# Pooled attention with a gated expert layer on one core: query rows summed by an accumulating DMA, exponentials issued head by head, a new order table

## Chip, cores and metric

One core of a Trainium2 chip. The metric is device microseconds of one execution of the whole program; the median of three timed runs of the kernel before is 1115.62 us (1115.05 to 1115.63).

## What is computed

The first half is attention with pooled queries, for 8 batches and 8 heads, 1152 positions, head size 64. The second half is a layer of 4 causal attention experts on the 576 pooled positions, of which every position takes the best 2.

```
q_pool = q.reshape(B, H, S // 2, 2, D).mean(axis=3)
scores = (q_pool @ k.T) / sqrt(D);  scores -= max;  a = exp(scores)
x      = (a / (sum(a) + 1e-9)) @ v                      # 8 x 576 x 512
logits = x @ w_gate                                     # best 2 of 4, softmax over them
for e in range(4):                                      # causal attention of expert e
    ye   = softmax(causal((x @ wq[e]) @ (x @ wk[e]).T / 8)) @ (x @ wv[e]) @ wo[e]
    out += gate[e] * ye
```

The mean over two query rows is computed as a sum; the factor of one half goes into the scale of the exponential (0.0625 where the reference has 0.125).

## The kernel before

Two heads make a pair, and 32 pairs (p) are worked off one after the other. A pair's two heads lie in the two halves of the 128 partitions. Precision is kept by splitting each fp32 operand into a high part in fp32r (`qh`, `kh`) and the rest (`ql`, `kl`); three products and one row that subtracts the maximum make a score.

For every pair:

- SyncE loads the raw queries `qraw` (both rows of each pooled pair: 128 partitions x 2 x 576, one buffer), the raw keys `kraw` in three pieces (512, 512, 128; the first pair in 3 x 384) and the values `v` in three (`f_loadq`, `f_loadk`, `f_loadv`).
- `f_prepq` makes `qh` and `ql` in two pieces of 256 and 320 columns: VectorE sums the two query rows into a PSUM bank (L559), ScalarE casts that to `qh` (L388) and copies a 64x64 corner into `QD`, VectorE subtracts `qh` from the bank and writes `ql` (L392). Only then is the bank free.
- `f_prepk` makes `kh` on ScalarE (L388) and `kl` on GpSimd (L396).
- `f_max` and `f_mxs` compute the scores of high parts alone on TensorE (L377, L368) and VectorE takes their row maxima (L633). `f_rows` turns these into the row `RM`.
- `f_st` computes the transposed scores (L377, four terms for each of 9 key chunks and 2 halves of the queries, `QB` = 256 and 320 columns); ScalarE writes the exponentials into SBUF tiles `pt` (L723). In the half of 256 columns two chunks share a PSUM bank per head, so a group is two chunks and two heads, four exponentials; in the other half it is one chunk and two heads.
- `f_av` multiplies them with `v` (L384); GpSimd adds the `pt` tiles of a half up (`pool_tt`, L396), or VectorE folds some of them into `part` instead (`fold_in`, L774). `f_xfin` and `g_norm` divide by the sum and write `x` as high and low part.

After every fourth pair one batch of the expert layer starts, and is worked off between the pairs that follow (`start_moe`; its exponentials are at L1104 and its causal mask is on GpSimd at L1124). The last batch has only the tail of the program beside it.

TensorE works in three arrangements, and the letters are those of the code: A, two row halves (L377); B, two column halves (L384, L821); C, the full array (L368).

The order of all instructions is set while the program is written. Each piece of work is a generator (`Flow`), and a planner in the main loop keeps a modelled clock for each engine (`emit`), with costs and semaphore delays as constants. It takes the next piece by readiness, arrangement and priority; the priorities come from a table of tuples, `PLAN`, of which a row applies to half a pair of progress (`row`). A booked DMA lands, in the planner, 0.65 us + bytes / 250 GB/s + 1.0 us after its issue. Each engine then runs its own list in that order, and waits where it must.

Of the kernel before, what the change touches and what calls it, by code (L numbers as in the profile page):

```python
# [1316 lines left out]
```

## Time and profile before

| what | value |
|---|---|
| median of three runs | 1115.62 us |
| the profiled execution, its own time | 1115.2 us |
| its span, first to last instruction | 1113.5 us |
| TensorE busy | 1090.7 us, 98% |
| VectorE busy | 925.1 us, 83% |
| GpSimd busy | 821.6 us, 74% |
| ScalarE busy | 655.4 us, 59% |
| DMA queue of SyncE | 68.29 MB, 19.1% of 16 engines' span |

The time is 1.7 us longer than the span. A matmul on two halves is two instructions that run side by side, so its rate is read from the start of one pair to the start of the next, and the busy times of neighbours overlap. A wait that TensorE sees at the weights of the next matmul (PEld) is in part hidden behind the matmul that still runs.

### The profile page before, as it was taken

Reading aid. Unit: us, or ns where it says so; the run is one execution under the profiler, and the core shown is the slowest. Engines: PE = TensorE matmul, PEld = TensorE weight load, DVE = VectorE, ACT = ScalarE, POOL = GpSimd, SP = SyncE. Lnnn points to the kernel's source line nnn. Section 1 sums busy time; section 2 is a strip of 40 time slices with the busy share of each in tenths; the row PEclk is TensorE's granted clock in tenths of the full one; section 3 lists DMA queues with packets and bytes.
Section 4 is the critical chain, followed back from the end, with each engine's and each line's share of the span. In section 5 each row is a group of like instructions: output and inputs, shape, how many; then the busy total and the mean of one; then the engine's idle time right before and its main releaser. Section 6 shows DMA issues by size and latency. Waiting matters only on the chain.

```text
span 1113.5 us, 29538 instructions
## 1 busy us (share of the span) xinstructions
PE 1090.7 (98%) x11184; PEld 877.2 (79%) x11184; DVE 925.1 (83%) x2159; ACT 655.4 (59%) x2067; POOL 821.6 (74%) x759
## 2 busy tenths in 40 slices
PE   6999999999999999999999999999999999999997
PEld 5777798778987888777887878778888867987785
DVE  8999969888798877988879787887888888685876
ACT  4776637575375744667446674567636766366534
POOL 4699948999189981999739996489865999278812
PEclk9999999999999999999999999999999999999999
DMA  5232202222021221212212031130221213010011
GB/s 168 83 117 84 89 32 66 66 66 85 20 81 51 63 84 41 78 44 66 84 40 89 24 101 47 51 108 2 94 74 66 66 26 123 22 31 2 1 39 48
DMA packets 41903, 70.32 MB, mean 63 GB/s; under 512 B 6688, under 2 KB 25120, under 8 KB 41760
## 3 DMA queue, kind: packets, MB, share of 16 engines
q1 hardware_dynamic: 41616, 68.29, 19.1%
q8 instruction: 88, 1.44, 0.5%
q14 instruction: 55, 0.45, 0.1%
q10 hardware_dynamic: 144, 0.13, 0.0%
HBM read 58.73 MB, written 9.44 MB: 61 GB/s over the span
## 4 chain that ended last, share of the span: by engine, by line
PE 84%; DVE 9%; POOL 3%; ACT 2%; issue 1%; DMA 0%; SPq 0%; DVEq 0%; POOLq 0%; ACTq 0%
PE gen L377 39%; PE gen L384 26%; PE gen L368 18%; DVE PM L633 3%; POOL pt L396 2%; ACT pt L723 2%; DVE gen L1060 1%; PE gen L821 1%; DVE part L774 1%; DVE pt L392 1%; POOL pt L1124 1%; DVE gen L836 1%; DMA qraw<-in_qT 0%; DVE gen L392 0%; DVE OL L392 0%
## 5 line engine op out<-in xcount | busy, mean ns | idle before, releaser
L396 POOL TENSOR_TENSOR pt<-pt,pt 128x512 f32<-128x512 f32 (+3 forms) x501 | 678.3, 1360 | 63.1 <-PE gen L384 17.1
L633 DVE TENSOR_REDUCE PM<-gen 128x1 f32<-128x512 f32 (+3 forms) x678 | 409.6, 658 | 84.9 <-PE gen L377 67.1
L723 ACT ACTIVATE pt<-gen 128x320 f32<-128x320 f32 (+1 forms) x1152 | 373.9, 435 | 57.7 <-PE gen L377 52.4
L384 PE MATMUL gen<-pt,v 128*64 128x320 f32 (+4 forms) x2752 | 343.9, 401 | 0.9 <-POOL pt L1124 0.7
L384 PEld LDWEIGHTS gen<-pt,v 128*64 128x64 f32 (+1 forms) x2752 | 187.9, 137 | 124.1 <-issue 4.3
L377 PE MATMUL gen<-qh,kh 64*128 64x320 f32 (+1 forms) x1152 | 238.2, 310 | 3.6 <-ACT pt L723 2.5
L377 PE MATMUL gen<-qh,kl 64*128 64x320 f32 (+1 forms) x1152 | 226.2, 299 | 0.0
L377 PE MATMUL gen<-RM,ON 64*128 64x320 f32 (+1 forms) x1152 | 217.5, 292 | 0.0
L377 PE MATMUL gen<-ql,kh 64*128 64x320 f32 (+1 forms) x1152 | 217.4, 292 | 0.0
L377 PEld LDWEIGHTS gen<-qh,kh 64*128 64x128 f32 x1152 | 162.8, 185 | 25.9 <-ACT pt L723 6.5
L377 PE MATMUL gen<-kh,qh 64*128 64x512 f32 (+2 forms) x768 | 151.9, 373 | 7.4 <-ACT qh L388 7.0
L377 PEld LDWEIGHTS gen<-ql,kh 64*128 64x128 f32 x1152 | 156.4, 186 | 0.0
L377 PEld LDWEIGHTS gen<-RM,ON 64*128 64x128 f32 x1152 | 156.3, 186 | 0.0
L377 PEld LDWEIGHTS gen<-qh,kl 64*128 64x128 f32 x1152 | 153.6, 186 | 2.6
L774 DVE TRANSPOSE_TENSOR_REDUCE part<-pt 128x20 f32<-128x640 f32 (+1 forms) x174 | 135.5, 789 | 17.9 <-POOL pt L396 17.7
L396 POOL TENSOR_TENSOR kl<-kraw,kh 128x512 fp32r<-128x512 f32 (+2 forms) x96 | 95.9, 1019 | 26.8 <-PE gen L377 23.1
L377 PEld LDWEIGHTS gen<-kh,qh 64*128 64x128 f32 x768 | 89.2, 188 | 25.5 <-issue 9.5
L975 POOL TENSOR_TENSOR gate<-v,gate 128x20 f32<-128x20 f32 x7 | 1.6, 231 | 144.9 <-DVE gate L975 144.9
L368 PE MATMUL gen<-x,WH 128*128 128x320 f32 (+1 forms) x512 | 105.0, 299 | 0.8 <-DVE x L392 0.8
L368 PEld LDWEIGHTS gen<-x,WH 128*128 128x128 f32 x512 | 82.1, 188 | 5.6 <-issue 3.0
L1060 DVE CUSTOM_DVE_ANT_0 gen<-gen,mqk 64x288 f32<-64x288 f32 (+4 forms) x160 | 74.1, 504 | 7.8 <-PE gen L377 6.7
L368 PE MATMUL gen<-x,WL 128*128 128x320 f32 (+1 forms) x256 | 75.6, 295 | 0.0
(120 smaller groups left out, 1472.7 us busy)
## 6 DMA issues: line engine op xcount, KB each, us to landing
v<-in_vP SPq DMA_DIRECT2D x96, 192.0 KB
qraw<-in_qT SPq DMA_DIRECT2D x31, 576.0 KB
kraw<-in_kT SPq DMA_DIRECT2D x62, 256.0 KB
out<-ob SPq DMA_DIRECT2D x28, 256.0 KB
kraw<-in_kT SPq DMA_DIRECT2D x31, 64.0 KB
RM<-nt SPq DMA_DIRECT2D x124, 1.2 KB
wst<-in_wall SPq DMA_DIRECT2D x8, 193.0 KB
MRM<-nt SPq DMA_DIRECT2D x56, 1.2 KB
```

The costliest lines, as they stand in the source:

```text
L368: nc.tensor.matmul(o, lhsT, rhs, start=start, stop=stop)
L377: nc.tensor.matmul(o(j), l(HEAD[j]), r(HEAD[j]), start=i == 0, stop=i == len(terms) - 1)
L384: nc.tensor.matmul(o(HEAD[j]), l(j), r(j), start=start, stop=stop)
L392: nc.vector.tensor_tensor(o, a, b, op=op)
L396: nc.gpsimd.tensor_tensor(o, a, b, op=op)
L633: nc.vector.tensor_reduce(pm[:, i:i + k, t], ps[:, :n * k].rearrange("p (c n) -> p c n", c=k), axis=AX.X, op=ALU.max)
L723: nc.scalar.activation(pts[i][:, j, :qn], st[j][:, qn * i:qn * i + qn], AF.Exp, scale=0.0625)
L774: nc.vector.tensor_reduce(out, src.rearrange("p a (b r) -> p a b r", r=32), axis=AX.X, op=ALU.add, apply_transpose=True)
L821: nc.tensor.matmul(den[HEAD[j], 400:400 + k], fold, part[:, m, j * k:j * k + k], start=True, stop=True)
L836: nc.vector.transpose(den[:, :n].rearrange("p (a b) -> p a b", b=32), r9[:, :k].unsqueeze(2).to_broadcast([128, k, 32]))
L1060: nc.vector.tensor_tensor_reduce(p, p, mqk[:m, 384 + m - w:384 + m], 1.0, LOW, ALU.add, ALU.max, pm[:m, j, c, i:i + 1])
L1124: nc.gpsimd.affine_select(out=sq, in_=sq, compare_op=ALU.is_ge, fill=0.0, base=0, pattern=[[0, 2], [1, kn]], channel_multiplier=-1)
```

## The change

1. `qraw` holds one row (128 x 576) and has two buffers. SyncE loads the first query row of a pair; a new step `f_addq` on GpSimd issues a DMA that adds the second row from HBM into the same tile (`accum_op=ALU.add`). The planner books 0.8 us of GpSimd for that (`SWC`).
2. `f_prepq` no longer uses VectorE or PSUM: ScalarE casts the summed tile to `qh` in one piece of 576 columns and makes both corners of `QD`; GpSimd makes `ql` in one piece.
3. The first pair is loaded as two separate tiles, in two pieces each, so four DMAs in place of two; VectorE adds them as before.
4. The exponentials of a group are issued head by head (first head, all chunks; second head, all chunks) and not chunk by chunk, in `f_st` and in `f_mst`, and the planner lets them start when the whole group's matmuls are done.
5. `PLAN` has new numbers in all of its rows.

```diff
+SWC = 0.8
-    r_qraw = ring("qraw", [128, 2, SQ], F32, 1)
+    r_qraw = ring("qraw", [128, SQ], F32, 2)
     def f_loadq(p):
-        mv(q.ap, qT[p], [], [q])
-        spawn("prepq", f_prepq(p, q))
+        mv(q.ap, qT[p][:, 0, :], [], [q])
+        spawn("addq", f_addq(p, q))
     def load_first():
-                mv(q[:, :, sl[t]], qT[0][:, :, sl[t]], [], [qs[t]])
+                for i, x in enumerate((q, q1)):
+                    mv(x[:, sl[t]], qT[0][:, i, sl[t]], [], [qs[t]])
-                dve_tt(q[:, 0, sl[t]], q[:, 0, sl[t]], q[:, 1, sl[t]], ALU.add, n, [qs[t]], [qs[t]])
+                dve_tt(q[:, sl[t]], q[:, sl[t]], q1[:, sl[t]], ALU.add, n, [qs[t]], [qs[t]])
...
+    def f_addq(p, q):
+        yield lambda: on(True, q.rw, pool())
+        nc.gpsimd.dma_start(q.ap, qT[p][:, 1, :], accum_op=ALU.add)
+        emit("POOL", SWC, [], [q], 4 * 128 * SQ / 250e3)
+        spawn("prepq", f_prepq(p, q))
     def f_prepq(p, q):
-        for i, (a, n) in enumerate(QB):
-            qs, c = r_gen.new(), slice(a, a + n)
-            nc.vector.tensor_reduce(qs[:, :n], q[:, :, c].rearrange("p a q -> p q a"), axis=AX.X, op=ALU.add)
-            act_copy(qh[:, c], qs[:, :n], n, [qs], [qh])
...
-            dve_tt(ql[:, c], qs[:, :n], qh[:, c].bitcast(F32), ALU.subtract, n, [qs, qh], [ql])
-            qs.free()
+        yield lambda: on(("row", 0, 0) in flag, q.rw, act(), r_qh.avail(), QD[p % 2].ru)
+        act_copy(qh.ap, q.ap, SQ, [q], [qh], False)
+        for j in range(2):
+            o = 64 * NQF * 2 * (1 - j)
+            act_copy(QD[p % 2][HEAD[j], 64 * j:64 * j + 64], q[HEAD[j], o:o + 64], 64, [q], [QD[p % 2]], False)
+        yield lambda: on(True, qh.rw, r_ql.avail(), pool())
+        pool_tt(ql.ap, q.ap, qh.bitcast(F32), ALU.subtract, SQ, [q, qh], [ql])
+        q.free()
     def f_st():
-                    for i, c in enumerate(cs):
-                        for j in range(2):
+                    for j in range(2):
+                        for i, c in enumerate(cs):
                             nc.scalar.activation(pts[i][:, j, :qn], st[j][:, qn * i:qn * i + qn], AF.Exp, scale=0.0625)
-                            emit("ACT", qn / 1200 + 0.055, [subs[i]], [pts[i]], late=0.05, U=[st[j]])
+                            emit("ACT", qn / 1200 + 0.055, [st[j]], [pts[i]], late=0.05)
 PLAN = [
-    (0.2, 0.6, 0.45, 1, 1, 1.2, 0.12, 0.04, 0, 4.05, 3.9, 4.6, 4.1, 2, 2, 0),
+    (0.05, 0.45, 0.45, 5, 2, 2.0, 0.25, 0.02, 4, 4.5, 2.9, 4.05, 4.1, 6, 99, 0),
...
```

What the new order does is seen in the engines' lists. Three places follow; in each the numbers behind the names count buffers and tiles.

VectorE's list, at the end of the first pair's row maxima (`PM0`, from the score banks `gen`) and the start of the second's (`PM1`); `qraw`, `ql` and `qh` belong to the second pair. Before:

```order
L559 TENSOR_REDUCE gen_27_296<-qraw_2_190 128x256
L633 TENSOR_REDUCE PM0_99<-gen_28_300 128x1
L633 TENSOR_REDUCE PM0_99<-gen_29_301 128x1
L392 TENSOR_TENSOR ql_2_295<-gen_27_296,qh_2_294 128x256
L559 TENSOR_REDUCE gen_32_331<-qraw_2_190 128x320
L633 TENSOR_REDUCE PM0_99<-gen_33_335 128x1
L633 TENSOR_REDUCE PM0_99<-gen_34_336 128x1
L659 TENSOR_REDUCE NM_105<-PM0_99 128x5 x2
L392 TENSOR_TENSOR ql_2_295<-gen_32_331,qh_2_294 128x320
L633 TENSOR_REDUCE PM1_100<-gen_37_371 128x1
```

and with the change:

```order
L635 TENSOR_REDUCE PM0_99<-gen_26_274 128x1
L635 TENSOR_REDUCE PM0_99<-gen_29_311 128x1
L635 TENSOR_REDUCE PM0_99<-gen_30_312 128x1
L661 TENSOR_REDUCE NM_105<-PM0_99 128x5 x2
L635 TENSOR_REDUCE PM1_100<-gen_31_321 128x1
L635 TENSOR_REDUCE PM1_100<-gen_32_322 128x1
```

The four instructions that prepare the second pair's queries are gone from VectorE, and the maxima follow each other.

GpSimd's list at the same place. Before:

```order
L396 TENSOR_TENSOR kl512_4_213<-kraw_4_164,kh512_4_205 128x512
L396 TENSOR_TENSOR kl128_1_245<-kraw_6_203,kh128_1_243 128x128
L396 TENSOR_TENSOR pt_1_264<-pt_1_264,pt_2_265 128x2x256
L396 TENSOR_TENSOR pt_1_264<-pt_1_264,pt_3_307 128x2x256
L396 TENSOR_TENSOR pt_1_264<-pt_1_264,pt_4_308 128x2x256
```

and with the change:

```order
L397 TENSOR_TENSOR kl512_4_218<-kraw_4_165,kh512_4_208 128x512
L558 DMA qraw_3_193<-in_qT 128x576
L558 DMA qraw_4_198<-in_qT 128x576
L397 TENSOR_TENSOR kl128_1_258<-kraw_6_216,kh128_1_256 128x128
L397 TENSOR_TENSOR ql_2_309<-qraw_3_193,qh_2_269 128x576
L558 DMA qraw_5_319<-in_qT 128x576
L397 TENSOR_TENSOR pt_1_279<-pt_1_279,pt_2_280 128x2x256
```

Three accumulating DMAs (pairs 2 to 4) and one `ql` stand ahead of the first sum of `pt` tiles.

ScalarE's list at the first exponentials. Before:

```order
L388 CAST RM0_95<-gen_20_239 65x384
L388 CAST kh512_6_262<-kraw_7_229 128x512
L723 ACTIVATE pt_1_264<-gen_25_266 128x256
L723 ACTIVATE pt_1_264<-gen_26_267 128x256
L723 ACTIVATE pt_2_265<-gen_25_266 128x256
L723 ACTIVATE pt_2_265<-gen_26_267 128x256
L388 CAST qh_2_294<-gen_27_296 128x256
```

and with the change:

```order
L389 CAST RM0_95<-gen_22_252 65x384
L389 CAST qh_2_269<-qraw_3_193 128x576
L389 CAST QD1_102<-qraw_3_193 64x64 x2
L725 ACTIVATE pt_1_279<-gen_27_281 128x256
L725 ACTIVATE pt_2_280<-gen_27_281 128x256
L725 ACTIVATE pt_1_279<-gen_28_282 128x256
L725 ACTIVATE pt_2_280<-gen_28_282 128x256
L389 CAST kh512_6_327<-kraw_7_235 128x512
```

The cast of the second pair's queries, which waits for an accumulating DMA, now stands ahead of the first exponentials, and both exponentials of the first head's bank come before those of the second's.

## Rows read from the trace of the kernel before

**Rows 1.** The profile's first part: busy time, share of the span and instructions of each engine.

```profile
PE 1090.7 (98%) x11184; PEld 877.2 (79%) x11184; DVE 925.1 (83%) x2159; ACT 655.4 (59%) x2067; POOL 821.6 (74%) x759
```

**Rows 2.** Busy time of each engine by stretch of the program: stretch in us, its length, busy us and instructions of TensorE, its weight loads, VectorE, ScalarE and GpSimd, the granted TensorE clock, the share of the DMA engines, GB/s.

```profile
0.00:25.00 25.00, 16.48 (x114) 12.78 (x115) 22.09 (x59) 12.50 (x35) 10.72 (x24) 1.00 0.58 187
25.00:50.00 25.00, 24.55 (x255) 18.25 (x251) 24.11 (x48) 15.48 (x48) 19.96 (x15) 1.00 0.24 81
50.00:100.00 50.00, 49.39 (x526) 37.85 (x528) 49.22 (x89) 37.72 (x117) 43.13 (x32) 1.00 0.36 112
...
200.00:300.00 100.00, 98.58 (x987) 80.19 (x984) 80.13 (x185) 55.09 (x177) 75.65 (x65) 1.00 0.18 61
```

**Rows 3.** Waits in the first stretch, 7 to 110 us: engine and line, what it waited for, us in total, times, the longest.

```profile
POOL kl L396 <- PE gen L377: 8.0, 4, 3.7
...
PEld gen L377 <- DVE PM L633: 4.3, 15, 0.8
...
PE gen L377 <- DVE PM L633: 0.7, 2, 0.5
```

**Rows 4.** TensorE's instructions in order of time, at 94 us: start, us from the first start to the last end, line, operation, tiles, shape, count, idle time before them and what ended it.

```profile
93.55 0.40 PE L377 MATMUL gen<-kh,qh 64*128 64x512 f32 x2
94.45 0.39 PE L377 MATMUL gen<-qh,kh 64*128 64x256 f32 x2 [0.50 <-DVE PM L633]
```

**Rows 5.** All engines in order of time in the first 21 us, the columns as in rows 4 (SPq is SyncE's queue of DMA issues).

```profile
1.24 0.70 SPq L413 DMA_DIRECT2D qraw<-in_qT  x1
...
2.61 0.58 SPq L413 DMA_DIRECT2D qraw<-in_qT  x1
...
5.16 0.99 POOL L396 TENSOR_TENSOR kl<-kraw,kh 128x384 fp32r<-128x384 f32 x1
5.51 0.99 DVE L392 TENSOR_TENSOR qraw<-qraw 128x320 f32<-128x320 f32 x1 [0.93 <-DMA qraw<-in_qT]
...
6.75 0.43 DVE L392 TENSOR_TENSOR qraw<-qraw 128x256 f32<-128x256 f32 x1 [0.24 <-DMA qraw<-in_qT]
...
7.05 1.49 PE L377 MATMUL gen<-kh,qh 64*128 64x384 f32 x6 [7.05 <-ACT qh L388]
...
7.77 7.06 DVE L633 TENSOR_REDUCE PM<-gen 128x1 f32<-128x384 f32 x15 [0.59 <-PE gen L377]
...
18.01 0.62 PE L377 MATMUL gen<-RM,ON 64*128 64x256 f32 x2
...
18.46 1.21 ACT L723 ACTIVATE pt<-gen 128x256 f32<-128x256 f32 x4 [1.64 <-PE gen L377]
...
18.74 0.70 DVE L559 TENSOR_REDUCE gen<-qraw 128x256 f32<-128x512 f32 x1
...
20.28 0.41 DVE L392 TENSOR_TENSOR ql<-gen,qh 128x256 fp32r<-128x256 f32 x1
```

**Rows 6.** Groups by line and shape: instructions, busy us in total and mean ns of one, then idle time of the engine before them.

```profile
L396 POOL TENSOR_TENSOR pt<-pt,pt 128x640 f32<-128x640 f32 x210 | 328.6, 1566 | 18.5 <-ACT pt L1104 6.5
...
L774 DVE TRANSPOSE_TENSOR_REDUCE part<-pt 128x20 f32<-128x640 f32 x119 | 98.0, 831 | 10.7 <-POOL pt L396 10.6
...
L396 POOL TENSOR_TENSOR kl<-kraw,kh 128x512 fp32r<-128x512 f32 x62 | 79.1, 1289 | 24.6 <-PE gen L377 23.1 <-ACT pt L723 1.1
...
L559 DVE TENSOR_REDUCE gen<-qraw 128x320 f32<-128x640 f32 x31 | 25.8, 833 | 0.0
...
L559 DVE TENSOR_REDUCE gen<-qraw 128x256 f32<-128x512 f32 x31 | 21.6, 697 | 7.9 <-ACT pt L723 7.9
...
L392 DVE TENSOR_TENSOR ql<-gen,qh 128x320 fp32r<-128x320 f32 x31 | 14.3, 460 | 1.0 <-ACT QD L388 0.8
...
L392 DVE TENSOR_TENSOR ql<-gen,qh 128x256 fp32r<-128x256 f32 x31 | 12.4, 401 | 0.1
```

**Rows 7.** Waits from 110 to 1060 us, TensorE (PE), its weight loads (PEld) and ScalarE, the columns as in rows 3.

```profile
PE gen L377 <- ACT pt L723: 2.3, 4, 0.7
PE gen L368 <- DVE PM L633: 1.3, 5, 0.3
...
PEld gen L377 <- ACT pt L723: 6.0, 16, 1.1
PEld gen L368 <- DVE PM L633: 3.2, 8, 0.5
...
PEld gen L377 <- DVE PM L633: 0.3, 1, 0.3
...
ACT x L388 <- DVE gen L392: 56.7, 52, 2.8
ACT qh L388 <- DVE gen L559: 22.2, 28, 1.6
```

**Rows 8.** TensorE in order of time where it changes from arrangement A to C, the columns as in rows 4.

```profile
503.17 0.41 PE L377 MATMUL gen<-ql,kh 64*128 64x320 f32 x2
503.32 0.41 PE L377 MATMUL gen<-RM,ON 64*128 64x320 f32 x2
503.66 0.80 PE L368 MATMUL gen<-kh,QD 128*128 128x512 f32 x3
```

**Rows 9.** The chain of waits that ended last, in order of time, first 110 us: start, us, what.

```profile
1.24 4.25 DMA qraw<-in_qT
```

**Rows 10.** ScalarE's last exponentials of a shared group in the tail, the columns as in rows 4.

```profile
1097.07 1.21 ACT L1104 ACTIVATE pt<-gen 128x320 f32<-128x320 f32 x4 [0.24 <-PE gen L377]
```

More of the change, by code (lines that the diff above doesn't have):

```diff
@@ L509, in load_first @@
     def load_first():
-        ks, q, qh, ql = [r_kraw.new() for _ in range(3)], r_qraw.new(), r_qh.new(), r_ql.new()
+        ks, (q, q1), qh, ql = [r_kraw.new() for _ in range(3)], [r_qraw.new() for _ in range(2)], r_qh.new(), r_ql.new()
         qs, sl = [Res(None) for _ in Q0], [slice(a, b) for a, b in Q0]
@@ L521, in load_first @@
                 n = sl[t].stop - sl[t].start
-                dve_tt(q[:, 0, sl[t]], q[:, 0, sl[t]], q[:, 1, sl[t]], ALU.add, n, [qs[t]], [qs[t]])
-                act_copy(qh[:, sl[t]], q[:, 0, sl[t]], n, [qs[t]], [QP[t]], False)
+                dve_tt(q[:, sl[t]], q[:, sl[t]], q1[:, sl[t]], ALU.add, n, [qs[t]], [qs[t]])
+                act_copy(qh[:, sl[t]], q[:, sl[t]], n, [qs[t]], [QP[t]], False)
                 j, o = 1 - t, NQF * 128 * t
-                act_copy(QD[0][HEAD[j], 64 * j:64 * j + 64], q[HEAD[j], 0, o:o + 64], 64, [qs[t]], [QD[0]], False)
+                act_copy(QD[0][HEAD[j], 64 * j:64 * j + 64], q[HEAD[j], o:o + 64], 64, [qs[t]], [QD[0]], False)
         for t in (0, None, 1, 2):
@@ L528, in load_first @@
                 for i in range(2):
-                    pool_tt(ql[:, sl[i]], q[:, 0, sl[i]], qh[:, sl[i]].bitcast(F32), ALU.subtract,
+                    pool_tt(ql[:, sl[i]], q[:, sl[i]], qh[:, sl[i]].bitcast(F32), ALU.subtract,
                             sl[i].stop - sl[i].start, [qs[i], QP[i]], [ql])
@@ L534, in load_first @@
             ks[t].free()
-        for r, xs in ((qh, QP), (q, qs)):
+        for r, xs in ((qh, QP), (q, qs), (q1, qs)):
             r.w, r.we = max((x.w, x.we) for x in xs)
@@ L539, in load_first @@
         q.free()
+        q1.free()
         flag.add(("QD", 0))
@@ L551, in spawn_max @@
         spawn("mxs", f_mxs(p), prio)
-    def f_prepq(p, q):
-        yield lambda: on(("row", 0, 0) in flag, q.rw, dve(), r_qh.avail(), r_ql.avail(), QD[p % 2].ru)
-        qh, ql = r_qh.new(), r_ql.new()
-        for i, (a, n) in enumerate(QB):
-            yield lambda: on(True, q.rw, dve(), r_gen.avail())
-            qs, c = r_gen.new(), slice(a, a + n)
-            nc.vector.tensor_reduce(qs[:, :n], q[:, :, c].rearrange("p a q -> p q a"), axis=AX.X, op=ALU.add)
-            emit("DVE", 2 * n / 960 + 0.07, [q], [qs])
-            yield lambda: rdy("ACT", qs.rw)
-            act_copy(qh[:, c], qs[:, :n], n, [qs], [qh])
-            j = 1 - i
-            o = 64 * (NQF * 2 * (1 - j)) - a
-            act_copy(QD[p % 2][HEAD[j], 64 * j:64 * j + 64], qs[HEAD[j], o:o + 64], 64, [qs], [QD[p % 2]])
-            if i:
-                QH[p] = qh
-                flag.add(("QD", p))
-                q.free()
-            yield lambda: rdy("DVE", qh.rw)
-            dve_tt(ql[:, c], qs[:, :n], qh[:, c].bitcast(F32), ALU.subtract, n, [qs, qh], [ql])
-            qs.free()
+    def f_addq(p, q):
[3 more added lines that the diff above has]
+        spawn("prepq", f_prepq(p, q))
+    def f_prepq(p, q):
+        yield lambda: on(("row", 0, 0) in flag, q.rw, act(), r_qh.avail(), QD[p % 2].ru)
+        qh = r_qh.new()
+        act_copy(qh.ap, q.ap, SQ, [q], [qh], False)
+        for j in range(2):
+            o = 64 * NQF * 2 * (1 - j)
+            act_copy(QD[p % 2][HEAD[j], 64 * j:64 * j + 64], q[HEAD[j], o:o + 64], 64, [q], [QD[p % 2]], False)
+        QH[p] = qh
+        flag.add(("QD", p))
+        yield lambda: on(True, qh.rw, r_ql.avail(), pool())
+        ql = r_ql.new()
+        pool_tt(ql.ap, q.ap, qh.bitcast(F32), ALU.subtract, SQ, [q, qh], [ql])
+        q.free()
         QL[p] = ql
@@ L710, in f_st @@
                     pts, st = [r_pt.new() for _ in cs], [r_gen.new() for _ in range(2)]
-                    qh, ql, subs = QH[p], QL[p], [Res(None) for _ in cs]
+                    qh, ql = QH[p], QL[p]
                     for i, c in enumerate(cs):
@@ L719, in f_st @@
                                (lambda r: ON[r], lambda r: rm[r, q0 + r.start:q0 + qn + r.start])],
-                              [kh, kl, qh, ql, rm], st + [subs[i]])
-                    for i, c in enumerate(cs):
-                        for j in range(2):
+                              [kh, kl, qh, ql, rm], st)
+                    for j in range(2):
+                        for i, c in enumerate(cs):
                             nc.scalar.activation(pts[i][:, j, :qn], st[j][:, qn * i:qn * i + qn], AF.Exp, scale=0.0625)
-                            emit("ACT", qn / 1200 + 0.055, [subs[i]], [pts[i]], late=0.05, U=[st[j]])
+                            emit("ACT", qn / 1200 + 0.055, [st[j]], [pts[i]], late=0.05)
                     for j in range(2):
@@ L1089, in f_mst @@
                 at = []
-                subs = [Res(None) for _ in g]
-                for i, c in enumerate(g):
+                for c in g:
                     kn, (f, w) = min(128, SQ - 128 * c), span(c)
@@ L1096, in f_mst @@
                            (lambda r: kh[r, kc], lambda r: ql[r, qc]), (lambda r: ON[r, :kn], lambda r: rm[r, qc])],
-                          [kh, kl, qh, ql, rm], st + [subs[i]])
+                          [kh, kl, qh, ql, rm], st)
                     o += qn - w
                     at.append(o)
-                for c, pt_, o, sub in zip(g, pts, at, subs):
-                    for j in range(2):
+                for j in range(2):
+                    for c, pt_, o in zip(g, pts, at):
                         kn, f = min(128, SQ - 128 * c), span(c)[0]
@@ L1104, in f_mst @@
                         nc.scalar.activation(pt_[:kn, j, f:qn], st[j][:kn, o - n:o], AF.Exp, scale=0.125)
-                        emit("ACT", n / 1200 + 0.055, [sub], [pt_], late=0.05, U=[st[j]])
+                        emit("ACT", n / 1200 + 0.055, [st[j]], [pt_], late=0.05)
                 for j in range(2):
```

128 rows, old and new, of the table PLAN are left out of this document.

## Prediction, made before the change was run

> **What bounds the kernel now.** I read the page's busy times first. TensorE is busy 98% of the span and no other engine over 83% [rows 1]. So time is gained only where TensorE stands still, changes its arrangement, or has not begun. The stretches come next: after the first 25 us TensorE is busy 24.55 us of 25 and 49.39 of 50, and between 200 and 300 us 98.58 of 100 [rows 2]. But VectorE is nearly as full at the start: 22.09 + 24.11 + 49.22 = 95.4 us of the first 100, and only 80.13 of 100 later [rows 2]. In the first four pairs, with no expert work between them, two engines are the bound together. The reader is to see in the waits of that stretch that the weight loads stood 4.3 us for row maxima, in 15 waits, and that 0.7 us of such waits show on TensorE itself [rows 3]. One of them in order of time: a pair of score matmuls starts at 93.55, the next only at 94.45, and half a microsecond of it is idle, ended by VectorE's maximum [rows 4].
>
> The profiled execution took 1115.2 us: a span of 1113.5 and 1.7 around it. That is 0.4 under the median of the runs shown, and the sum is made against 1115.2. About 0.2% (2.2 us) is what a measurement of this kernel can tell from no change.
>
> **The change, part by part.** TensorE's list holds the same matmuls in both kernels, so no work leaves the bound; all gains are waits and arrangement changes.
>
> *The start.* The first half of the queries now comes as two DMAs. Its issue takes 0.70 us in one piece, the second half's 0.58 [rows 5]; with four issues, the first half's last is out about 0.6 us later and the second half's about 1.2 us. The first add takes 0.99 us for 320 columns and ends at 6.50, while the second takes 0.43 for 256; GpSimd's subtraction ran from 5.16 to 6.15 [rows 5]. So the first add stood until GpSimd was through and then ran 0.35 us, and data that land 0.6 us later cost it nothing. (The Trainium skill, SBUF — State Buffer, "Who interferes with whom", says a VectorE instruction with two SBUF inputs contends with a GpSimd one that reads SBUF, and the one that started first holds the port to its end; the trace agrees with 0.99 against 0.43 us. By landing times alone I would have added 0.6 us here too.) The second add stands in front of all maxima on VectorE, which start at 7.77 and then run 15 in 7.06 us without a break [rows 5]. It ended at 7.18; with a landing 1.2 us later it ends at 8.4. I take +0.6, bounds 0 (the smaller transfers land as early as now) and +1.3.
>
> *VectorE in the first 100 us.* Each preparation loses two sums and two subtractions: 833 + 697 + 460 + 401 ns = 2.39 us [rows 6], and its listing shows them gone. Four preparations are 9.6 us. The new list folds 21 tiles in place of 19 up to the fifth pair's maxima, which gives back 2 x 0.83 = 1.7 [rows 6]. VectorE falls from 95 to about 87 of 100 us, near the load it has later; and from 110 to 1060 us the same wait for maxima at the score matmuls is 0.3 us in all [rows 7]. So most of 4.3 + 0.7 should go, except the start's own maxima, which run back to back in any order; I give them 2.0. That leaves −3.0, bounds −0.7 (what showed on TensorE itself) and −5.0.
>
> *The rest of the program.* VectorE loses 27 more preparations; in exchange it makes 14 folds more in the whole program (188 for 174). It was no bound there. What may help TensorE is PSUM: a preparation held a bank from the sum at 18.74 to the end of the subtraction at 20.69 [rows 5], twice per pair, 62 times 1.95 = 121 us of bank time that is now free. Head by head, the first head's bank is free after two exponentials and not three, 0.3 us (four in 1.21) earlier; and nothing starts later, since the four already began only when the second chunk's last matmuls, started at 18.01, were done [rows 5]. TensorE itself waited 2.3 us for exponentials and 1.3 for maxima from 110 to 1060 us, its loads 6.0 and 3.2 [rows 7]. I take −1.5, some 40% of what shows on TensorE; bounds −4.0 and +2.0, since a new order brings waits of its own.
>
> *Arrangement changes.* Counted over TensorE's whole list there are 202 before and 195 now. One costs what the step exceeds the steady one by: the pairs start 0.15 us apart, the change took from 503.32 to 503.66, so 0.19 us [rows 8]. 7 x 0.19 = −1.3, bounds 0 and −2.
>
> *GpSimd.* It gains 31 issues and 31 subtractions of 576 columns. Between 1289 ns (512) and 1566 (640) [rows 6] a subtraction is 1.43 us. No row shows a DMA issued from GpSimd; the nearest are SyncE's issue of 0.58 us [rows 5] below and GpSimd's longest sum, 1.57 us, above. I take the planner's 0.8, near SyncE's: 31 x 2.23 = 69 us. It loses 10 sums of 512 and 3 of 640 columns: 12.9 + 4.7. So 821.6 + 51 = 873 us [rows 1], with 240 idle. Covered by that idle time: 0. If the cover is gone, that is the third rival.
>
> *ScalarE* casts 576 columns once instead of twice, and loses 4 us in all; it idles 41%. Its wait of 22.2 us for VectorE's sums [rows 7] goes, and a wait for the accumulating DMA takes its place. The planner lets the cast follow 0.65 + 1.2 + 1.0 = 2.8 us after the issue. In the trace the first query load took 4.25 us to land, for 328 KB among other loads [rows 9]. I take 0: most casts stand well behind their DMA, and the second pair's, which is the tightest, stands behind a cast of `RM` that the maxima hold. Being late is the second rival. (A price that only a page has: The Trainium skill, DMA: Bandwidth & Descriptors, "Anatomy of one DMA — SWDGE (gpsimd) path", gives 2.0 us + bytes / 436 GB/s, 2.7 us for these 295 KB, an estimate; by it nothing waits. No run here shows it.)
>
> *The tail.* Head by head, the causal mask of a shared group's first chunk starts after three exponentials and not two, and four took 1.21 us [rows 10]: +0.3, bounds 0 and +0.8. The last output blocks stand in nearly the same order.
>
> Sum: 1115.2 + 0.6 − 3.0 − 1.5 − 1.3 + 0 + 0 + 0.3 = 1110.3. All lower bounds together give 1104, all upper ones 1118.6.
>
> **The rivals.**
>
> *VectorE's relief does not reach TensorE.* For it: TensorE reads 98% busy, and only 0.7 us of the early waits shows there [rows 1, 3]. Then 1115.2 + 0.6 − 0.7 − 1.3 + 0.3 = 1114.1, no change. The chance is 0.24. That head by head does nothing at all is part of it.
>
> *The accumulated rows land late, and ScalarE stands at its head.* Behind the cast on ScalarE stand exponentials, behind them TensorE for PSUM. It decides from landings over 2.8 us after the issue where the cast follows at once. Landing in 4.25 us as the first load did, each cast waits 1.45 us; at twice that, 5.7: 45 to 177 us on ScalarE, less the 22 that go. Of ScalarE's waits on VectorE (56.7 + 22.2) TensorE and its loads felt 2.3 + 6.0, a tenth [rows 7]. So +2 to +16; in the middle 1110.3 + 9 = 1119. Against it: the queries have two buffers and are mostly loaded a pair ahead. (A rule speaks for it: The Trainium skill, SBUF — State Buffer, "SBUF: two separate sides", says VectorE instructions in a two-port mode, such as an fp32 copy within SBUF, keep GpSimd from writing its descriptors. It would delay each landing by up to one such copy; VectorE's costly groups here are reductions, so I give the rule no chance beyond this rival's.) 0.09.
>
> *GpSimd becomes the bound of the first pairs.* It was busy 63.1 us from 25 to 100 us [rows 2], and waited 8.0 for TensorE [rows 3]. Three preparations add 6.7: 77.8 of 75 us, if no wait shrinks. It then runs 2.8 us over, and both of VectorE's gains are lost: 1110.3 + 3.0 + 1.5 + 2.8 = 1117.6, just slower. Against it: VectorE now takes more folds. 0.07.
>
> **How the numbers follow.** The forecast has 0.60, the rivals 0.24, 0.09 and 0.07. Most of the forecast's own values lie under 1113, which is faster; the first rival is within 0.2%; the other two are slower, 0.16. The range goes from 1104.5, where nearly all lower bounds meet, to 1119, the middle of the second rival.
>
> **What would show it.** In the changed profile: VectorE near 863 us (925.1 − 74 + 12) and GpSimd near 873; in the first 100 us VectorE under 90, and the weight loads' wait for maxima there under 2.5 us; the first matmul still at 7.05 and the first maximum near 8.4. Wrong would be: ScalarE waiting for a DMA at `qh` by more than 20 us in all (second rival), GpSimd without idle time from 25 to 100 us (third), or VectorE as light as said and TensorE as slow as before (first).

## The result, and the profile after

The changed kernel takes **1124.91 us** (median of 4 runs, 1124.25 to 1126.16) against 1115.57 (the kernel before, 4 runs): a ratio of 1.0086, 95% interval 1.0069 to 1.0104. It is slower, and outside the range given (1104.5 to 1119). The profiled execution has a span of 1123.1 us, 9.6 more than before.

Busy times and the two rows of the chain that ended last (shares of the span by engine, then by line), on the page of the changed kernel:

```profile
PE 1092.6 (97%) x11184; PEld 878.3 (78%) x11184; DVE 875.7 (78%) x2055; ACT 651.9 (58%) x2036; POOL 874.4 (78%) x808
...
PE 70%; POOL 12%; DVE 11%; issue 2%; DMA 2%; ACT 2%; SPq 0%; POOLq 0%; DVEq 0%; ACTq 0%
PE gen L378 31%; PE gen L369 20%; PE gen L385 19%; POOL pt L397 10%; DVE PM L635 5%; DVE part L776 2%; DMA qraw<-in_qT 2%; POOL pt L1125 1%; DVE gen L1062 1%; POOL kl L397 1%; ACT pt L725 1%; PE gen L823 1%; DVE WL L393 1%; DVE gate L977 1%; DMA kraw<-in_kT 0%
```

Before, the chain read:

```profile
PE 84%; DVE 9%; POOL 3%; ACT 2%; issue 1%; DMA 0%; SPq 0%; DVEq 0%; POOLq 0%; ACTq 0%
```

Against [rows 1], VectorE has 49 us less and GpSimd 53 us more, the way the diff says. The chain is where to look: it ran 84% over TensorE and 3% over GpSimd before, now 70 and 12, and 10 of the 12 are line L397 at `pt`, GpSimd's sums of exponentials. The reader is to see that GpSimd, 22% idle, lies on the path.

Stretches, the columns as in [rows 2] (TensorE, weight loads, VectorE, ScalarE, GpSimd, granted clock):

```profile
0.00:25.00 25.00, 17.09 (x110) 12.44 (x112) 21.90 (x58) 11.53 (x30) 14.61 (x28) 1.00 0.74 199
25.00:50.00 25.00, 25.00 (x273) 19.16 (x271) 23.54 (x47) 17.46 (x57) 21.52 (x17) 1.00 0.31 84
50.00:100.00 50.00, 45.94 (x469) 34.69 (x470) 48.16 (x78) 32.74 (x99) 45.49 (x35) 0.95 0.41 110
...
200.00:300.00 100.00, 98.63 (x995) 78.33 (x996) 74.32 (x171) 55.67 (x178) 85.41 (x76) 0.98 0.26 68
...
600.00:700.00 100.00, 98.89 (x1043) 79.90 (x1041) 79.62 (x171) 60.56 (x197) 94.48 (x83) 1.00 0.24 62
```

TensorE does well up to 50 us and loses in 50 to 100, where it was 49.39 us busy [rows 2]. From 200 to 300 GpSimd has 85.41 us for 75.65 before, and from 600 to 700 it is busy 94.48 us of 100.

Waits over the whole span, changed kernel (columns as in [rows 3]):

```profile
POOL gate L977 <- DVE gate L977: 128.2, 14, 21.2
...
ACT qh L389 <- DMA qraw<-in_qT: 37.0, 18, 4.4
...
DVE part L776 <- POOL pt L397: 27.2, 30, 3.7
```

The same rows before, over the whole span too:

```profile
POOL gate L975 <- DVE gate L975: 147.8, 13, 24.0
...
ACT qh L388 <- DVE gen L559: 26.8, 32, 1.8
DVE part L774 <- POOL pt L396: 17.7, 17, 3.6
```

`ACT qh`, the cast of the queries, waited 26.8 us for VectorE's sums (22.2 of them in the stretch of [rows 7]) and now waits 37.0 for the DMA. The third row is VectorE standing for GpSimd's sums: 27.2 us, for 17.7 before. The first decides what GpSimd's idle time is worth. The gate chooses the experts of a batch; the group of its first GpSimd instruction, before and in the change, shows how the wait is made up (busy us, mean ns, idle before):

```profile
L975 POOL TENSOR_TENSOR gate<-v,gate 128x20 f32<-128x20 f32 x7 | 1.6, 231 | 144.9 <-DVE gate L975 144.9
```

```profile
L977 POOL TENSOR_TENSOR gate<-v,gate 128x20 f32<-128x20 f32 x7 | 1.6, 225 | 123.9 <-DVE gate L977 123.9
```

Half of GpSimd's 292 us without work (1113.5 less 821.6) lay before 7 instructions, one for each batch but the last, some 21 us each; in the change they are some 18 us each.

One stall from its cause to its end, the chain of the changed kernel in order of time (start, us, what, at 224 to 240 us):

```profile
224.34 1.57 POOL pt L397 x2
...
227.32 2.86 POOL pt L397 x3
...
231.33 4.92 POOL pt L397 x5
...
236.32 1.02 POOL pt L397
...
237.91 0.84 DVE part L776
238.75 0.59 DVE PM L635
...
239.38 0.84 PE gen L369 x3
```

GpSimd adds up exponentials for 13 us with gaps of up to 1.4 us; its last sum lets VectorE fold, VectorE's maximum stands behind that fold, and TensorE behind the maximum. TensorE was busy 0.71 of 2 us there, and the granted clock fell behind it to its lower level, 1.2 GHz:

```profile
238.00:240.00 2.00, 0.71 (x4) 0.41 (x3) 2.00 (x4) 0.87 (x3) 2.00 (x3) 1.00 0.11 33
240.00:242.00 2.00, 1.98 (x23) 1.34 (x24) 1.93 (x7) 0.00 (x0) 2.00 (x3) 0.85 0.67 158
242.00:244.00 2.00, 2.00 (x14) 1.09 (x12) 1.90 (x6) 0.00 (x0) 2.00 (x2) 0.50 1.01 238
```

The largest stall, 91.95 to 97.16 us, began at VectorE's subtraction for the weights (L393, `WL`), which took 4.02 us while GpSimd issued a DMA and ran `kl`, `ql` and sums without pause; from there on the chain stays on VectorE up to 97.16. VectorE and then GpSimd, changed kernel, columns as in [rows 4]:

```profile
80.78 4.02 DVE L393 TENSOR_TENSOR WL<-wst,WH 128x386 fp32r<-128x386 f32 x1
```

```profile
79.57 0.90 POOL L558 DMA_DIRECT2D qraw<-in_qT  x1
80.18 1.60 POOL L397 TENSOR_TENSOR kl<-kraw,kh 128x512 fp32r<-128x512 f32 x1
81.43 1.72 POOL L397 TENSOR_TENSOR ql<-qraw,qh 128x576 fp32r<-128x576 f32 x1
```

### The profile page after: what moved, and what is told of

Its sections match the earlier page's. It is cut to its first block, busy times and chain, and to the rows that moved or that the text cites. A ratio compares the mean times of both kernels' runs of the same rounds, so it can differ in the third digit from the quotient of the medians.

```text
span 1123.1 us, 29516 instructions
## 1 busy us (share of the span) xinstructions
PE 1092.6 (97%) x11184; PEld 878.3 (78%) x11184; DVE 875.7 (78%) x2055; ACT 651.9 (58%) x2036; POOL 874.4 (78%) x808
## 4 chain that ended last, share of the span: by engine, by line
PE 70%; POOL 12%; DVE 11%; issue 2%; DMA 2%; ACT 2%; SPq 0%; POOLq 0%; DVEq 0%; ACTq 0%
PE gen L378 31%; PE gen L369 20%; PE gen L385 19%; POOL pt L397 10%; DVE PM L635 5%; DVE part L776 2%; DMA qraw<-in_qT 2%; POOL pt L1125 1%; DVE gen L1062 1%; POOL kl L397 1%; ACT pt L725 1%; PE gen L823 1%; DVE WL L393 1%; DVE gate L977 1%; DMA kraw<-in_kT 0%
## 5 line engine op out<-in xcount | busy, mean ns | idle before, releaser
L397 POOL TENSOR_TENSOR pt<-pt,pt 128x512 f32<-128x512 f32 (+4 forms) x488 | 667.7, 1374 | 40.5 <-PE gen L385 5.1
L378 PE MATMUL gen<-qh,kh 64*128 64x320 f32 (+1 forms) x1152 | 229.8, 312 | 4.8 <-DVE PM L635 2.5
L378 PE MATMUL gen<-qh,kl 64*128 64x320 f32 (+1 forms) x1152 | 218.1, 299 | 0.0
L378 PE MATMUL gen<-RM,ON 64*128 64x320 f32 (+1 forms) x1152 | 210.4, 292 | 0.0
L378 PEld LDWEIGHTS gen<-qh,kh 64*128 64x128 f32 x1152 | 155.8, 186 | 28.1 <-ACT pt L725 7.3
L776 DVE TRANSPOSE_TENSOR_REDUCE part<-pt 128x20 f32<-128x640 f32 (+1 forms) x188 | 143.4, 781 | 27.5 <-POOL pt L397 27.2
L378 PE MATMUL gen<-kh,qh 64*128 64x512 f32 (+2 forms) x768 | 149.4, 374 | 11.2 <-ACT qh L389 7.1
L378 PEld LDWEIGHTS gen<-ql,kh 64*128 64x128 f32 x1152 | 149.3, 186 | 0.0
L378 PEld LDWEIGHTS gen<-qh,kl 64*128 64x128 f32 x1152 | 146.1, 186 | 2.8
L397 POOL TENSOR_TENSOR kl<-kraw,kh 128x512 fp32r<-128x512 f32 (+2 forms) x96 | 103.0, 1104 | 21.0 <-PE gen L378 16.7
L378 PEld LDWEIGHTS gen<-kh,qh 64*128 64x128 f32 x768 | 88.3, 189 | 29.9 <-issue 11.2
L389 ACT COPY accs<-gen 128x256 f32<-128x256 f32 (+1 forms) x96 | 39.1, 407 | 70.6 <-PE gen L385 70.5
```

The costliest lines, as they stand in the source:

```text
L378: nc.tensor.matmul(o(j), l(HEAD[j]), r(HEAD[j]), start=i == 0, stop=i == len(terms) - 1)
L389: nc.scalar.copy(o, i)
L397: nc.gpsimd.tensor_tensor(o, a, b, op=op)
L776: nc.vector.tensor_reduce(out, src.rearrange("p a (b r) -> p a b r", r=32), axis=AX.X, op=ALU.add, apply_transpose=True)
```

## Experiments

The first question was whether the new operations cost or the new order does. "Lists in the same order" means that the planner's books are left alone and only the instructions named differ.

**Old order, new operations (e1, e2, e11).** The planner of before keeps booking its own sums; the instructions become those of the change.

```
+            nc.gpsimd.dma_start(q.t.ap, qT[p][:, 1, :], accum_op=ALU.add)   # where row one is booked as landed
...
-            nc.vector.tensor_reduce(qs[:, :n], q[:, :, c]..., op=ALU.add)
+            if not i: nc.scalar.copy(qh.ap, q.t.ap)
...
-            dve_tt(ql[:, c], qs[:, :n], qh[:, c]..., ALU.subtract, ...)
+            if i: nc.gpsimd.tensor_tensor(ql.ap, q.t.ap, qh..., op=ALU.subtract)
```

> The kernel before with its list of TensorE, and of every other engine, in the old order, into which only the accumulating DMA and the split from SBUF are put: 31 issues and 31 subtractions of 576 columns more on GpSimd, the sums and low parts of 31 preparations gone from VectorE, one cast for two on ScalarE; exponentials chunk by chunk, old table of numbers. Theory A (the new order has TensorE's idle time in it, the new operations cost nothing): 1111 to 1116 us, no slower than before, VectorE near 850 us busy. Rival B (GpSimd's extra 75 us and the rows that land 4.5 us after their issue are what costs): 1119 us or more, with ScalarE waiting some 30 us for the DMA at qh as in the change. Rival C (VectorE's 4.0 us subtraction of weights beside GpSimd's new work, with the half clock behind it, is the loss): 1117 to 1121, with a stall near 92 us and a granted clock under 1.00 there.

Measured: 1199.58 us, ratio 1.0755 (1.0737 to 1.0773), VectorE 864.2 and GpSimd 890.5 us busy. Rival B's sign, with ScalarE waiting 37.0 us at `qh`, but 84 us are far beyond its 1119; Theory A falls. VectorE waited 62.4 us for GpSimd's sums.

e2 has the exponentials head by head besides.

> As the first kernel of this set, and the exponentials of a group head by head, again in the old order of all else: all operations of the change, none of its order. Theory A (only the new order costs): within 2 us of the first kernel and not over 1116 us. If the order of the exponentials costs something by itself, 2 us or more above the first kernel, with more waits of TensorE's loads for exponentials than 7.7 us.

Measured: 1199.34 us, the same.

e11 is e1 without the line with `dma_start`.

> The first kernel of this study (the lists of before in the old order, with the preparation from SBUF), without its 31 accumulating DMAs: VectorE has 62 sums and 62 low parts less than before, GpSimd 31 subtractions more; the second query row is left out from the second pair on. If the old order gives no room on GpSimd for more work: 1120 to 1150 us, between the 1115.2 of before and 1199.6. If VectorE's relief reaches TensorE in any order: 1106 to 1112. If it needs the new order and GpSimd has room: 1113 to 1117.

Measured: 1147.45 us, 1.0290 (1.0275 to 1.0306), with VectorE at 864.0 and GpSimd at 862.6. VectorE is 61 us lighter than before and GpSimd 41 us busier, VectorE's waits for GpSimd's sums are 41.9 us, and the kernel is 32 us slower: in the old order, whose planner does not book GpSimd's new work, VectorE's relief does not make up for it. So the new operations need an order that was made with them; whether it has to be this one was not tried.

**New order, head by head undone (e4).** The two loops around the exponentials change places, for pairs and for experts.

```
-                    for j in range(2):
-                        for i, c in enumerate(cs):
+                    for i, c in enumerate(cs):
+                        for j in range(2):
                             nc.scalar.activation(pts[i][:, j, :qn], st[j]..., AF.Exp, scale=0.0625)
```

> The changed kernel with its lists in the same order, only the exponentials within a group of chunks back in the order chunk by chunk. Theory A: 1124 to 1126 us, since head by head frees a PSUM bank 0.3 us earlier and little hangs on it. If head by head gains what the prediction gave it, 1126 to 1128; if it costs, 1122 or less.

Measured: 1128.69 us, 1.0120 (1.0104 to 1.0136). Head by head gives 3.8 us here, by the medians; the lowest run without it (1126.48) is just above the highest with it (1126.16). In the old order, alone, by the opposite edit (e12):

> The kernel before, lists in the old order, only the exponentials of a group head by head. In the new order head by head gave 3.8 us (1128.7 without, 1124.9 with it). If it gives that by itself: 1110 to 1113 us, faster than both kernels. If it needs the order that was made for it: 1114.5 to 1117, no change.

Measured: 1114.61 us, 0.9995 (0.9985 to 1.0004): no change.

**New order, the accumulating DMA taken apart (e3, e5, e6, e7).**

```
-        nc.gpsimd.dma_start(q.ap, qT[p][:, 1, :], accum_op=ALU.add)
e3       (nothing)
e5+      nc.gpsimd.dma_start(scr, qT[p][:, 1, :64])
e6+      nc.sync.dma_start(q.ap, qT[p][:, 1, :])
```

> The changed kernel with its lists in the same order, its 31 accumulating DMAs left out (from the second pair on the output lacks the second query row of each pair): GpSimd loses 31 issues of 0.92 us and nobody waits for a landing. Theory A: 1121 to 1125 us, still slower than before, as only the unplanned stalls get shorter. Rival B: back at 1114 to 1117 us. Rival C: the stall at 92 us stays, since VectorE's subtraction still meets GpSimd's, so 1121 to 1124 with the granted clock at 0.5 after it.

Measured: 1108.71 us, 0.9943 (0.9928 to 0.9958). The 31 DMAs cost 1124.91 − 1108.71 = 16.2 us, and without them the kernel is 6.5 us faster than the kernel before (1115.20 beside these runs). `WL` at 81 us is short, in the kernel without the DMAs:

```profile
81.06 0.55 DVE L393 TENSOR_TENSOR WL<-wst,WH 128x386 fp32r<-128x386 f32 x1
```

> The changed kernel, lists in the same order; each of the 31 DMAs from GpSimd now writes 64 of the 576 columns, without accumulating, into a buffer that nobody reads (so the output lacks the second query row from the second pair on). GpSimd's issues stay, with no wait for the first row; no landing is waited for and hardly any data moves. The kernel without these DMAs took 1108.7 us, the changed one 1124.9. If the landing is what costs (late rows at ScalarE's head): 1108 to 1112 us. If GpSimd's time for the issues is what costs (28 us, and the sums of the exponentials late by it): 1119 to 1125.

Measured: 1118.05 us, 1.0029 (1.0017 to 1.0040), between the two answers: issues whose data nobody waits for cost 9.3 of the 16.2 us (1118.05 − 1108.71). GpSimd also waited 6.8 us there for the one small buffer.

> The changed kernel, lists in the same order; the second row comes at the same places by a plain DMA from SyncE into the same buffer (it overwrites the first, so the sum is left out), so GpSimd issues nothing, the same bytes move, and the cast still waits for the landing. If the landing is what costs: 1118 to 1125 us with ScalarE waiting some 30 us for the DMA at qh. If GpSimd's issues cost: 1108 to 1113.

Measured: 1109.27 us, 0.9953 (0.9938 to 0.9968). The same bytes from SyncE's queue cost 0.6 us over e3. ScalarE waited only 7.6 us at `qh`, so this clears the bytes and SyncE's queue, and the landing only in part.

For e7 a flow of its own issues the DMA, and GpSimd's time stays booked where it was:

```
+    def f_issq(p, q):
+        t0 = q.rw
+        yield lambda: t0
+        nc.gpsimd.dma_start(q.ap, qT[p][:, 1, :], accum_op=ALU.add)
...
     def f_addq(p, q):
-        nc.gpsimd.dma_start(q.ap, qT[p][:, 1, :], accum_op=ALU.add)
```

> The changed kernel complete, lists in the same order but for the 31 accumulating DMAs, each put forward in GpSimd's list to where the first row is booked as landed (where it already stood there it stays). GpSimd's work is the same. If the landing is what costs: 1112 to 1118 us, ScalarE's wait for the DMA at qh under 12 us. If GpSimd's time costs: 1122 to 1128, since the issues now may also stand for the first row ahead of sums.

Measured: 1123.54 us, 1.0074 (1.0059 to 1.0089). The waits, kernel with early issues:

```profile
DVE part L782 <- POOL pt L397: 40.0, 35, 3.7
...
POOL qraw L560 <- DMA qraw<-in_qT: 9.0, 3, 4.0
...
ACT qh L389 <- DMA qraw<-in_qT: 2.9, 2, 1.7
```

ScalarE's 37.0 us became 2.9 and the time fell by 1.4; the two intervals overlap. But the landing's price is not isolated by that: the early issues stand 9.0 us on GpSimd for the first row (4.6 in the change), and VectorE's waits for GpSimd's sums rose from 27.2 to 40.0 us. One wait was traded for another.

The run shows something else. VectorE's weight subtractions (`WL`) take 7.3 us in all, as before the change (7.4; 11.6 in the change), the granted clock stays at 1.00 up to the last 15 us, and ScalarE hardly waits. Still the kernel takes 14.8 us more than e3, in which VectorE's waits for sums are 19.1 us. So late sums can make a loss of nearly this size with the other three all but gone.

**GpSimd's time, more and less of it (e9, e10).** 

```
         nc.gpsimd.dma_start(q.ap, qT[p][:, 1, :], accum_op=ALU.add)
e9+      nc.gpsimd.dma_start(scr[:, o:o + 32], qT[p][:, 1, o:o + 32])
...
e10-     pool_tt(ql.ap, q.ap, qh.bitcast(F32), ALU.subtract, SQ, [q, qh], [ql])
e10+     emit("POOL", SQ * 0.0024 + 0.1, [q, qh], [ql])
```

> The changed kernel complete, lists in the same order, with a second small DMA behind each of the 31 on GpSimd (32 columns, into a buffer that nobody reads): some 31 x 0.57 = 18 us more on GpSimd, nothing else. If GpSimd's time is what costs, whatever it is spent on: without any issue 1108.7, with 17.7 us of them 1118.1, with the change's 28.1 us 1124.9, so half a microsecond for each; 1132 to 1136 us. If only the accumulating DMA itself or its landing costs: 1124 to 1127.

Measured: 1131.95 us, 1.0147 (1.0130 to 1.0164). Over four kernels that differ only in the DMAs issued from GpSimd (in the last two ScalarE also waits for their landing):

| kernel | GpSimd busy | its wait at the gate | VectorE's waits for its sums | time |
|---|---|---|---|---|
| no DMA from GpSimd (e3) | 847.6 us | 140.5 us | 19.1 us | 1108.71 us |
| small ones (e5) | 864.5 | 130.0 | 26.7 | 1118.05 |
| the change | 874.4 | 128.2 | 27.2 | 1124.91 |
| and 31 small ones more (e9) | 890.7 | 119.4 | 39.2 | 1131.95 |

(1131.95 − 1108.71) / (890.7 − 847.6) = 0.54 us for each microsecond on GpSimd; the single steps give 0.55, 0.69 and 0.43. The other half was covered: the wait at the gate is 21.1 us shorter in e9 than in e3, of 43.1 us more work. The two rows, e3 and e9:

```profile
POOL gate L976 <- DVE gate L976: 140.5, 13, 20.8
```

```profile
POOL gate L980 <- DVE gate L980: 119.4, 13, 19.5
```

> The changed kernel, lists in the same order, without GpSimd's 31 subtractions for the queries' low part (it is left out of the scores from the second pair on); the accumulating DMAs stay. GpSimd has 46.7 us less. If GpSimd's time costs, whatever it is spent on: 1103 to 1112 us, as without the DMAs or better. If a DMA issue is special (VectorE's standing behind it, or the landing): 1119 to 1125.

Measured: 1111.99 us, 0.9973 (0.9963 to 0.9983). The DMAs are all there, and 12.9 us of the 16.2 are gained without touching them. So GpSimd's time costs also where no DMA fills it. But its total does not set the time alone: GpSimd is busy 831.3 us here, 16 less than in e3, and the kernel takes 3.3 us more. Two of its waits:

```profile
ACT qh L391 <- DMA qraw<-in_qT: 18.6, 11, 4.3
...
DVE part L778 <- POOL pt L399: 9.7, 15, 1.7
```

VectorE waits less for sums than in e3, so the 3.3 us seem to be something else that the DMAs bring; ScalarE's wait for them and `WL` at 80.57 (2.64 us) are both left here, and nothing tells them apart.

**VectorE in GpSimd's place (e8).** The second row comes from SyncE, and VectorE adds.

```
-        nc.gpsimd.dma_start(q.ap, qT[p][:, 1, :], accum_op=ALU.add)
...
+        nc.vector.tensor_tensor(q[:, :DM], q[:, :DM], q.two, op=ALU.add)
+        nc.vector.tensor_tensor(q[:, DM:], q[:, DM:], q.three, op=ALU.add)
```

> The changed kernel complete, lists in the same order, but the second row comes by plain DMAs from SyncE into buffers of their own (the weights' and the output's) and VectorE adds the two rows, 512 and 64 columns, in place: 31 x 0.73 us (by the second add of the start, 0.43 us for 256 columns, and its step per column, an estimate) = 23 us more on VectorE and 28 us less on GpSimd. If the accumulating DMA is all that loses: 1109 to 1114 us, faster than both kernels. If VectorE is again too full in the first 100 us: 1114 to 1118.

Measured: 1143.42 us, 1.0259 (1.0243 to 1.0274). My price for the adds was wrong. Groups by shape, this kernel (busy us, mean ns):

```profile
L570 DVE TENSOR_TENSOR qraw<-qraw,qrest 128x64 f32<-128x64 f32 x31 | 36.1, 1163 | 0.0
L569 DVE TENSOR_TENSOR qraw<-qraw,qtwo 128x512 f32<-128x512 f32 x31 | 33.5, 1080 | 2.1 <-DMA qtwo<-in_qT 2.0
```

64 columns took longer than 512: 36.1 + 33.5 = 69.6 us in place of 23, so most of it was not the adding. The Trainium skill, SBUF — State Buffer, "Who interferes with whom", has the rule: a VectorE instruction with two SBUF inputs contends with a GpSimd one that reads SBUF. The trace agrees, with 1163 ns for 64 columns, near the length of one GpSimd instruction (1289 ns for `kl`, 1566 for a sum [rows 6]). How much of the 18.5 us over the change these adds cost, and how much the borrowed buffers, was not taken apart.

**The time bought back, complete (e13 to e16).** A rule after `fold_in` moves sums of exponentials from GpSimd to a fold on VectorE, into one slot more of the partial sums; GpSimd stays booked for them, so the rest of the order is the same. e13 takes them where the planner's own slots are full, e14 wherever there are partial sums. The expectations count 24, 37 and, for e16, 29 of them; the traces hold one less each, 23, 36 and 28.

```
-        if c and not fold_in(sacc, pt, n):
+        if c and not fold_in(sacc, pt, n) and not extra(sacc, pt, n):
             add_up(sacc, pt, 0, n, n, pool_tt)
+    def extra(sacc, pt, n):
+        part = PARTS.get(sacc)
+        if part is None or part.n > part.m or part.m < NSL: return False      # e13; e14 without the last
...
+        nc.vector.tensor_reduce(part[:, part.n, :2 * k]..., pt..., op=ALU.add, apply_transpose=True)
+        part.n += 1
...
```

> The changed kernel complete, lists in the same order but for 24 sums of exponentials (640 or 512 columns) that move from GpSimd to a fold on VectorE, into one slot more of the partial sums: GpSimd some 24 x 1.5 = 36 us less, about what the accumulating DMAs took, VectorE 24 x 0.78 = 19 us more. If GpSimd's time alone loses: 1109 to 1115 us, no slower than before. If the DMA itself or its landing carries a part that GpSimd's relief can't give back: 1116 to 1121. If VectorE is the bound again: 1122 or more.

Measured: **1106.08 us**, 0.9917 (0.9903 to 0.9930): faster than both kernels, with every operation of the change in it. Page and waits of this kernel:

```profile
PE 1083.0 (98%) x11184; PEld 874.5 (79%) x11184; DVE 887.1 (80%) x2078; ACT 651.9 (59%) x2036; POOL 839.0 (76%) x785
...
PE 86%; DVE 10%; DMA 1%; issue 1%; ACT 1%; POOL 1%; SPq 0%; DVEq 0%; ACTq 0%; POOLq 0%
```

```profile
POOL gate L992 <- DVE gate L992: 141.0, 13, 22.8
...
ACT qh L390 <- DMA qraw<-in_qT: 14.6, 10, 3.0
...
DVE part L777 <- POOL pt L398: 2.8, 4, 1.1
```

GpSimd has 35.4 us less than in the change, and the time is 18.8 us less: 0.53 for each. GpSimd's share of the chain is 1% for 12, VectorE's waits for its sums 2.8 us for 27.2. Of the rest of the relief, 12.8 us went into a longer wait at the gate (141.0 for 128.2). ScalarE's wait for the DMAs fell too, from 37.0 to 14.6 us, with the issues earlier, so this run alone does not part late sums from late landings.

> The same with 37 sums moved: GpSimd some 55 us less, VectorE 29 us more. If GpSimd's time alone loses: 1106 to 1113 us, faster than both kernels. If VectorE's added time counts as much: 1114 to 1120.

Measured: 1106.61 us, 0.9927 (0.9913 to 0.9940): within the range named, and no better than e13. With VectorE's waits for sums gone (2.9 us, 2.8 in e13), more relief buys nothing.

e15 is e14 with the early issues of e7, e16 the rule of e14 in the kernel before.

> As the one with 37 sums moved, and the accumulating DMAs put forward to where the first row is booked as landed, so that ScalarE hardly waits for them. If the landing still costs something: 1 to 2 us under the one without (as 1124.9 to 1123.5 in the changed kernel). If not: within 1 us of it.

Measured: 1108.49 us, 0.9939 (0.9926 to 0.9951): 1.9 us above the one without, which neither answer had. Here ScalarE's wait fell from 11.2 to 2.2 us and VectorE's waits for sums stayed (2.9 and 3.1), so what is left of the landing gives nothing back; what the 37.0 us of the change cost is not shown by it.

> The kernel before with the same rule, which moves 29 sums from GpSimd to VectorE there: GpSimd some 44 us less, VectorE 23 us more. If GpSimd's time lost something in the kernel before too: 1108 to 1113 us. If it was covered there, as the prediction took all of GpSimd's to be, and VectorE is the fuller one: 1115 to 1122.

Measured: 1116.93 us, 1.0014 (1.0005 to 1.0023), GpSimd 779.8 and VectorE 940.0 us busy. The kernel before gains nothing from the same rule, though VectorE's waits for sums fell from 17.7 to 7.9 us. Either GpSimd's time was covered there, or VectorE's 15 us more (its share of the chain is 16%, for 9) took back what the relief gave.

## Why the prediction was wrong

**The step that failed** is *GpSimd*: "So 821.6 + 51 = 873 us [rows 1], with 240 idle. Covered by that idle time: 0." The 873 was right (874.4), the cover was not. The change's issues cost 16.2 us for 26.8 us more on GpSimd, 0.54 for each microsecond over the four kernels of the table, and the kernel with 35 us taken off GpSimd elsewhere gets 18.8 back. Of the idle time I counted on, half lay in 7 long waits at the gate, and these took up about half of what was added. In between GpSimd works in blocks; an instruction put into a block delays the sums behind it, then VectorE's fold, and the maxima queued behind the fold, as the chain at 224 to 240 us shows.

*The start*, +0.6: 0. The second half's add still took 0.43 us, at 6.89 for 6.75, and the first maximum came at 7.81 for 7.77, not at 8.4; the first matmul at 7.09.

*VectorE in the first 100 us*, −3.0: almost nothing. The first four pairs have no expert work between them, so the end of their last exponential can be compared: 105.6 us before, 105.4 without the DMAs (e3). VectorE has 93.6 us of the first 100 in the change and 93.8 in e3, not under 90; up to 105.5 us, 17 folds for 13, three maxima more and longer weight subtractions (`WL` and `OL`, 12.1 us for 10.2 in e3) filled most of what the sums left. The loads waited 6.3 us for maxima, not under 2.5. So the first rival was right about this stretch. Over the whole program VectorE came out at 875.7 us, not at 863; 4 of the 13 us between are the `WL` subtractions (11.6 us for 7.4). In the change the fourth pair ends at 109.6, behind the stall at 92 us.

*The rest of the program*, −1.5, *arrangement changes*, −1.3, and *the tail*, +0.3: too small together. Without the DMAs' cost the kernel is 6.5 us faster than before and only 0.2 of it comes in the first four pairs. Head by head may carry 3.8 us of it, measured in the kernel with the DMAs. The arrangement changes were not tried alone. That the forecast's gains, 4.9 us net, come near these 6.5 is luck: the largest term gave almost nothing, and the small ones gave more.

*GpSimd's issues*, 0.8 us each: 0.92 measured; *the low part*, 1.43: 1.51. Small.

*ScalarE*, 0: the landing took 4.5 us, near the second rival's 4.25, and ScalarE waited 37.0 us, past my mark of 20. The mark does not decide by itself: issues without any landing cost 9.3 us (e5), 31 small issues more cost another 7.0 with ScalarE's wait hardly changed (38.5 us in e9), and with that wait gone the time moved by 1.4 us (e7, in which sums came later). So the second rival had the sign, and the time lies in its 1112 to 1126, but its mechanism is not the main one; that late landings have a share of a few microseconds is not excluded. The third had the right engine, priced for 25 to 100 us alone; GpSimd had 8 us idle there, and what it lost came over the whole program.

What stays open: why head by head gives 3.8 us in one order and nothing in the other; and how the 16.2 us divide. Late sums can make most of such a loss alone (e7); late landings, VectorE's long subtractions beside GpSimd and the stretches at half clock were never taken away one at a time. e9 has all of these and sums as late as e7's (39.2 and 40.0 us), and takes 8.4 us longer.

## What to carry to other kernels

Idle time covers new work only if it lies where the work is put. Before costing an addition at nothing, list what that engine's idle time consists of: a few long waits at one place took up only half of the work added here, and an engine with a quarter of its time free can be the late one in the blocks between. The longest new wait on a page is not the price either. Take it away and look at what the other waits did meanwhile, for the early issues here traded one wait for another; then relieve the engine that the chain names.

## What was not expected of the hardware

- A DMA issue occupies GpSimd by itself. Groups of the changed kernel by shape (busy us, mean ns, idle before), then, from its page, the row of its DMA issues (KB each, median us from issue to landing):

```profile
L397 POOL TENSOR_TENSOR ql<-qraw,qh 128x576 fp32r<-128x576 f32 x31 | 46.7, 1508 | 4.0 <-ACT qh L389 3.0 <-ACT pt L725 1.0
L558 POOL DMA_DIRECT2D qraw<-in_qT x31 | 28.1, 916 | 10.3 <-DMA qraw<-in_qT 4.6 <-ACT pt L725 4.5 <-DMA kraw<-in_kT 1.2
```

```profile
qraw<-in_qT POOLq DMA_DIRECT2D x31, 288.0 KB, 4.5
```

An issue with 576 columns a row took 916 ns, one with 64 columns 571 (17.7 us for 31, e5). Such a record can overlap its neighbour's: 31 issues of 32 columns, each straight behind another issue, read 901 ns each in e9, while GpSimd's busy time rose by 16.3 us, 0.53 each. The landing took 4.5 us for 288 KB and 2.1 for 32 KB. By the Trainium skill, DMA: Bandwidth & Descriptors, "Anatomy of one DMA — SWDGE (gpsimd) path", it would be 2.7 and 2.1 (estimates from its 2.0 us + bytes / 436 GB/s). The trace agrees for the small transfer and not for the large accumulating one.

- The granted clock fell to 0.50 behind each of the two long stalls (92 to 97 and 238 to 240 us), so TensorE ran on at its lower level after the stall had ended. Behind the first:

```profile
98.00:100.00 2.00, 2.00 (x20) 2.00 (x20) 2.00 (x4) 0.87 (x4) 1.92 (x2) 0.50 0.04 8
```

In e13, with neither stall, it is 1.00 up to the last stretch.
